# A 32-byte tile in front and two padded tiles: every tile of an attention and expert kernel moves in SBUF

## The chip, the cores and the metric

The kernel runs on one core of a Trainium2 chip. The metric is the device time of one execution in microseconds (us). Before the change it is 664.34 us, the median of 3 runs (664.32 to 665.79).

## What is computed

The reference is a linear attention with complex decay over 4 batches, 8 heads, 768 steps and 48 dimensions, followed by a mixture of 8 experts on its output.

```python
for t in range(S):                       # a = a_re + i a_im, scaled to a magnitude of at most 0.999
    new_re = ar * S_re - ai * S_im
    new_im = ar * S_im + ai * S_re
    S_re, S_im = (new_re + kv, new_im)   # kv = outer(k[t], v[t])
    y[t] = q[t] @ S_re
x = y as [3072 tokens, 384]
noisy_logits = x @ w_gate + log1p(exp(x @ w_noise)) * noise
# each token goes to its two best experts, with softmax weights over the two
out[mask] += top2_w * (maximum(x[mask] @ w1[e], 0) @ w2[e])   # w1[e]: 384x1024, w2[e]: 1024x384
```

## The kernel before, in words

**Attention (the first 250 us or so).** The 768 steps are cut into 6 groups of 128, so with 4 batches there are 24 tiles. Running sums of the logarithm and the angle of the decay are matmuls with triangular constants (`tri_t`, `tri_l`, `mask`; L365, L389), queries and keys are turned by transposes against `ident` (L414), scores are matmuls (L425), and outputs add the scores' part and the state's (L478, L476). Each output tile is turned back (L491), a gate picks two experts for each token, and POOL scatters the tokens' rows `xr` into the experts' slots `xs` in DRAM (L570). The order of all these instructions on each engine is written out by hand in `ORDER`.

**Experts (from about 271 us).** Every expert has 832 slots, cut into a window 0 of 320 and a window 1 of 512. For an expert the kernel loads its rows into `xga` and `xgb`, turns them, and keeps them as `x0` and `x1` (one tile for each third of the 384 dimensions). [...]

- First product, L763 (`mm1`): for each of 8 blocks f of the hidden size, 9 matmuls add up in PSUM. The stationary operand is `w1` (128 columns of it), the moving one is `x1` (512 columns; 448 for expert 0) or `x0` (320 columns; 256 where an expert's last 64 slots of window 0 are empty, which the kernel asks at run time). So a window has 72 matmuls. ACT takes the maximum with zero into `h` (L772), DVE the rest of it (L776).
- Second product, L832 (`mm2`): an output tile j of 128 slots adds up 24 matmuls. The stationary operand is 128 columns of `h0` (tiles 0, 1) or `h1` (tiles 3 to 6), the moving one 384 columns of `w2`. Tile 2 has 64 slots and 16 matmuls (L838), and only where those slots are used; for expert 0 tile 6 is such a half tile too. DVE weighs and adds the result into `ao` (L846), and POOL sends it to the output's rows (L847).

The order on PE from expert 2 on: first product of window 1, first product of window 0, second product of tiles 3 to 6, then (2,) 0 and 1.

**Where tiles lie.** A tile takes the same bytes in each of the 128 partitions, rounded up to a multiple of 32. Pools on the left side stack up from byte 8,320 of a partition: the constants (`cp`) up to 21,216; behind it `pf` (the attention's working tiles), later replaced by `mp0`; then `mp1` and `mp2` for the experts. Pools on the right side (`pa`, `pq`: queries, keys, values, scores, `xr` and more) end at the top, whatever stands on the left. A new pool's tile that lies over a tile of a closed pool waits for that one's last reader. Positions before, as the remainder of the first byte on division by 64:

| tiles | pool | first byte | remainder |
|---|---|---|---|
| ident, tri_t, tri_l, mask, tri_b, ones_b, none, xga | cp | 8,320 to 13,248 | 0 |
| zero, wg, nz | cp | 18,080 to 20,384 | 32 |
| re, im, t0, ee, tf | pf | 21,216 to 73,440 | 32 |
| raw (loaded weights) | mp0 | 21,216 to 29,408 | 32 |
| w1 of even-numbered experts | mp0 | 33,504 to 61,792 | 32 |
| x0, h0 | mp0 | 41,824 to 83,808 | 32 |
| w2 | mp1 | 86,368 to 107,872 | 32 |
| w1 of odd-numbered experts | mp1 | 110,944 to 131,424 | 32 |
| ao, xgb, lim | mp2 | 135,520 to 152,672 | 32 |
| lo, x1, ex, h1, xt | mp2 | 152,704 to 202,240 | 0 |
| all larger tiles | pa, pq | 87,744 to 225,728 | 0 |

The slices that the matmuls take of `w1`, `w2`, `x` and `h` begin whole multiples of 256 bytes behind their tile's first byte, so they have the tile's remainder.

Of the kernel before, what the change touches and what calls it, by code (L numbers as in the profile page):

```python
# [9 lines left out]
F32 = mybir.dt.float32  # L10
# [67 lines left out]
def kernel(  # L78
# [14 lines left out]
    E = w_gate.shape[1]  # L93
# [16 lines left out]
    xd = nc.dram_tensor("xd", [N, DM + E], F32, kind="Internal").ap()  # L110

    cp = ctx.enter_context(tc.tile_pool(name="cp", bufs=1))

    def ones_where(t, cmp, pattern, cm, base, fill):
        nc.gpsimd.affine_select(out=t, in_=t, pattern=pattern, compare_op=cmp, fill=fill,
                                base=base, channel_multiplier=cm)
# [171 lines left out]
    def key(name, ins):  # L288
        K.setdefault(name, []).append(ins)
        return ins  # L290
# [322 lines left out]
    def load_x(e, w, dst):  # L613
        if w == 0 and e not in TAILS:
            ds = [key(f"S14.{e}{w}", nc.sync.dma_start(dst[:, 0:2], x3[e, 0:256].rearrange("(p j) r -> p j r", j=2))),
                  key(f"S14.{e}{w}", nc.sync.dma_start(dst[0:64, 2], x3[e, 256:320]))]
            first.extend(ds)
            for d in ds:
                for s in late:
                    tc.declare_no_dep(d.ins, s.ins, reason="slots behind the first 320")  # L620
        elif e == 0:
            key(f"S14.{e}{w}", nc.sync.dma_start(dst, x3[e, 320:CAP].rearrange("(j p) r -> p j r", p=128)))
        else:

            n = WIN[w][1]
            x = blocks(dst, n)
            o = CAP - n if w == 0 or e not in TAILS else 0
            for a in range(4):
                asked.append(nc.sync.dma_start(x[32 * a:32 * a + 32], x3[e, o:o + n, 96 * a:96 * a + 96].rearrange("(t p) r -> p t r", p=32)))
            if w == 0:  # L630
                return
            EX[e] = ex = mt([128, 7, 16], F32, name="ex", bufs=2)
            m = 6 if e in TAILS else 4
            asked.append(nc.sync.dma_start(ex[:, 0:m], x3[e, o:o + 128 * m, DM:ROW].rearrange("(m p) r -> p m r", p=128)))
            if e in TAILS:
                nc.sync.dma_start(ex[0:64, 6], x3[e, CAP - 64:CAP, DM:ROW])

    def blocks(t, n):
        return t.rearrange("p j r -> p (j r)")[:, 0:3 * n].rearrange("p (t r) -> p t r", r=96)
# [15 lines left out]
    W1, W2, XW, HT, GW, OX, EX, DONE = {}, {}, {}, {}, {}, {}, {}, {}  # L655
    where = {}

    def mt(shape, dt, name, **kw):

        at_ = len(mpools) - 1  # L660
        if name.startswith(("raw", "h0", "x0", "gw", "ox")) or name.startswith("w1") and name.endswith("0"):
            at_ = 0
        elif name.startswith(("w1", "w2")):
            at_ = 1
        return where.setdefault(name, mpools[at_]).tile(shape, dt, name=name, **kw)
# [240 lines left out]
    for g in range(NG):  # L906
        for lo, hi in ((0, B),) if g < NG - 2 else ((0, B - 1), (B - 1, B)):
            for f, k, x in ((glog, 0, "gl"), (gturn, 2, "gl"), (gpick, 4, "gd"), (gdis, 10, "gd")):
                at(pos(B * g + hi + .5 + P[x], f"G{k}.{part(g, lo)}"), f, g, lo, hi)
            at(pos(behind_key(B * g + hi + .5 + P["gd"], f"G12g.{part(g, lo)}"), f"S13.{part(g, lo)}"), gscat, g, lo, hi)  # L910
        if g == NG - 4:
            at(pos(behind_key(B * g + hi + .5 + P["gd"], f"G12g.{g}"), "S14.00"), load_x, 0, 0, xga)
# [36 lines left out]
    for kk in range(KD):  # L949
        at(max(fpos + .002, PLACE[f"P21.00{kk}"]), x_T, 0, 0, (kk,))  # L950
        at(max(qpos + .003, PLACE[f"P21.10{kk}"]), x_T, 1, 0, (kk,))
    at(max(fpos + .003, PLACE["S14.10"], PLACE[f"P21.00{KD - 1}"] + .001), load_x, 1, 0, xga)
    for f in range(KF):
        at(PLACE[f"P22.00{f}"], mm1, 0, 0, (f,))
# [21 lines left out]
    mp = mpools[-1]  # L976
# [3 lines left out]
    xgb = mp.tile([128, 4, ROW], F32, name="xgb")  # L980
    for a in ao:
        nc.vector.memset(a, 0.0)
    lim = mp.tile([128, E], F32, name="lim")
    nc.gpsimd.iota(lim, pattern=[[N, E]], base=CAP, channel_multiplier=0, allow_small_or_imprecise_dtypes=True)
    load_x(0, 1, xgb)
    mm2(0, 0)
    ON = {"G0": "P", "G1": "A", "G2": "P", "G5": "A", "G7": "A", "G9": "A", "G10": "P"}
# [239 lines left out]
```

## Time and profile before

| | |
|---|---|
| time, median of 3 runs | 664.34 us |
| profiled execution | 671.12 us, span 669.3 us |
| PE busy | 633.1 us, 95% of the span |
| weight load (PEld) busy | 566.3 us, 85% |
| DVE busy | 430.4 us, 64% |
| ACT busy | 327.5 us, 49% |
| POOL busy | 175.6 us, 26% |
| granted TensorE clock, mean | 0.994 |

The span is the time from the first to the last instruction of the profiled execution. PEld is TensorE's load of a stationary operand, which runs beside the matmul before it. Matmuls overlap, so the distance between their starts tells what one costs, not its duration in the trace.

### The profile page before, as it was taken

Reading aid. Unit: us, or ns where it says so; the run is one execution under the profiler, and the core shown is the slowest. Engines: PE = TensorE matmul, PEld = TensorE weight load, DVE = VectorE, ACT = ScalarE, POOL = GpSimd, SP = SyncE. Lnnn points to the kernel's source line nnn. Section 1 sums busy time; section 2 is a strip of 40 time slices with the busy share of each in tenths; the row PEclk is TensorE's granted clock in tenths of the full one; section 3 lists DMA queues with packets and bytes.
Section 4 is the critical chain, followed back from the end, with each engine's and each line's share of the span. In section 5 each row is a group of like instructions: output and inputs, shape, how many; then the busy total and the mean of one; then the engine's idle time right before and its main releaser. Section 6 shows DMA issues by size and latency. Waiting matters only on the chain.

```text
span 669.3 us, 13780 instructions
## 1 busy us (share of the span) xinstructions
PE 633.1 (95%) x5312; PEld 566.3 (85%) x5312; DVE 430.4 (64%) x957; ACT 327.5 (49%) x556; POOL 175.6 (26%) x185
## 2 busy tenths in 40 slices
PE   1599999999999999999999999999999999999995
PEld 0378788888688979898998998998998999999995
DVE  7789999999987578445465535736545744634311
ACT  7799989999954633314233403504413504503300
POOL 3000004242614136016124124024123312312311
PEclk9999999999999999999999999999999999999998
DMA  8588875756596366815647157156355725401211
GB/s 263 161 286 253 230 205 177 227 174 162 173 267 190 103 210 210 209 37 150 168 107 191 58 131 233 49 144 209 96 109 166 188 65 156 142 36 60 69 37 35
DMA packets 97049, 102.68 MB, mean 153 GB/s; under 512 B 60815, under 2 KB 78096, under 8 KB 96968
## 3 DMA queue, kind: packets, MB, share of 16 engines
q1 hardware_dynamic: 87624, 74.08, 40.2%
q0 software_dynamic: 9344, 27.54, 11.6%
q8 instruction: 48, 0.79, 0.5%
q14 instruction: 33, 0.27, 0.1%
HBM read 70.93 MB, written 31.60 MB: 153 GB/s over the span
## 4 chain that ended last, share of the span: by engine, by line
PE 83%; ACT 6%; DVE 4%; DMA 3%; issue 2%; POOL 0%; another core or an unknown queue 0%; SPq 0%; POOLq 0%; ACTq 0%; DVEq 0%
PE po L832 30%; PE ph L763 28%; PE ptr L414 4%; PE psc L425 4%; PE cum L365 2%; PE pY L476 2%; PE pY L478 2%; PE pG L439 2%; ACT t L296 2%; PE po L838 2%; PE psc L763 2%; PE cum L389 2%; PE cum L491 1%; PE cum L503 1%; ACT ee L296 1%
## 5 line engine op out<-in xcount | busy, mean ns | idle before, releaser
L832 PE MATMUL po<-w2h,h 128*128 128x384 f32 x752 | 194.6, 337 | 0.0
L763 PE MATMUL ph<-x,w1h 128*128 128x512 f32 (+3 forms) x720 | 185.5, 346 | 0.4 <-issue 0.4
L763 PEld LDWEIGHTS ph<-x,w1h 128*128 128x128 f32 x720 | 126.0, 188 | 16.8 <-DVE ox L726 0.8
L832 PEld LDWEIGHTS po<-w2h,h 128*128 128x128 f32 x752 | 136.7, 188 | 0.1
L832 PE MATMUL po<-w2l,h 128*128 128x384 f32 x376 | 126.7, 337 | 0.0
L763 PE MATMUL ph<-x,w1l 128*128 128x512 f32 (+3 forms) x360 | 124.4, 345 | 0.0
L847 POOL DMA_INDIRECT out_dram<-ao,ox x52 | 52.5, 1009 | 255.9 <-DVE ao L846 200.7
L776 DVE SCALAR_TENSOR_TENSOR h<-ph,h 128x256 fp32r<-128x256 f32 (+3 forms) x152 | 69.6, 481 | 67.3 <-ACT h L772 51.6
L570 POOL DMA_INDIRECT xs<-xr,sl x48 | 57.5, 1198 | 185.6 <-DMA im<-in_a_dram 93.1
L772 ACT ACTIVATE h<-ph 128x512 fp32r<-128x512 f32 (+2 forms) x112 | 55.6, 502 | 98.6 <-PE ph L763 86.1
L846 DVE SCALAR_TENSOR_TENSOR ao<-po,ex,ao 128x384 f32<-128x384 f32 (+1 forms) x42 | 25.8, 615 | 87.8 <-PE po L832 87.5
L763 PEld LDWEIGHTS ph<-x,w1l 128*128 128x128 f32 x360 | 67.9, 188 | 7.9
L832 PEld LDWEIGHTS po<-w2l,h 128*128 128x128 f32 x376 | 70.6, 188 | 0.1
L685 ACT CAST w2h<-raw 128x768 fp32r<-128x768 f32 x32 | 26.3, 833 | 84.2 <-PE po L832 73.8
L807 POOL DMA_INDIRECT ao<-out_dram,ox x49 | 55.5, 1134 | 37.1 <-DMA out_dram<-ao,ox 20.8
L743 ACT CAST x<-xt 128x512 fp32r<-128x512 f32 (+1 forms) x39 | 20.9, 546 | 54.1 <-DVE xt L742 52.2
L425 PEld LDWEIGHTS psc<-qT,kT 112*64 112x64 f32 x768 | 36.2, 137 | 6.5 <-issue 5.4
L425 PE MATMUL psc<-qT,kT 112*64 112x128 f32 (+1 forms) x768 | 41.2, 251 | 0.4 <-issue 0.3
L686 DVE TENSOR_TENSOR w2l<-raw,w2h 128x768 fp32r<-128x768 f32 x32 | 30.2, 955 | 12.9 <-ACT w2h L685 12.0
L478 PE MATMUL pY<-am,v 128*48 128x128 f32 x384 | 36.6, 273 | 0.9 <-DVE am L427 0.5
L427 DVE TENSOR_TENSOR am<-psc,mask 128x512 f32<-128x512 f32 x48 | 32.3, 682 | 6.2 <-PE psc L425 2.6
L296 ACT ACTIVATE t<-t 128x768 f32<-128x768 f32 (+1 forms) x42 | 31.6, 763 | 1.9 <-DVE bad L339 1.7
(227 smaller groups left out, 938.8 us busy)
## 6 DMA issues: line engine op xcount, KB each, us to landing
raw<-in_moe_w_dram SPq DMA_DIRECT2D x24, 512.0 KB
raw<-in_moe_w_dram SPq DMA_DIRECT2D x32, 384.0 KB
qk<-in_qk_dram SPq DMA_DIRECT2D x24, 384.0 KB
v<-in_v_dram SPq DMA_DIRECT2D x24, 288.0 KB
xgb<-xs SPq DMA_DIRECT2D x28, 192.0 KB
out_dram<-zero SPq DMA_DIRECT2D x12, 384.0 KB
re<-in_a_dram SPq DMA_DIRECT2D x11, 384.0 KB
im<-in_a_dram SPq DMA_DIRECT2D x11, 384.0 KB
```

The lines of the kernel that those rows point to most:

```text
L296: phases[i].append(nc.scalar.activation(*args, **kw))
L425: key(f"P5{'ab'[half]}.{n}", nc.tensor.matmul(p[o:o + 64, j, s:], KT[n][:, h, s:s + 64], QT[n][:, h, s:], start=True, stop=True, skip_grou ...
L427: LAST['am'] = nc.vector.tensor_mul(AM[n][:, 4 * half:4 * half + 4, :].rearrange("p (i r) t -> p i r t", r=2), p.rearrange("p (i r) t -> p ...
L478: x = nc.tensor.matmul(o, V[n][:, H + i if r else h, :], AM[n][:, h, :], start=not g, stop=True, skip_group_check=True)
L570: d = key(f"L{b}{kk}.{part(g, lo)}", nc.gpsimd.indirect_dma_start(out=xs, out_offset=bass.IndirectOffsetOnAxis(ap=sl[:, kk, b:b + 1], axis=0),
L686: d = key(f"D{name}", nc.vector.tensor_tensor(lo, raw_t, hi.bitcast(F32), op=OP.subtract))
L763: LAST['m'] = key(f"P22.{e}{w}{f}", nc.tensor.matmul(p[:, :c], W1[e, kk][i][:, f * 128:(f + 1) * 128], XW[w, kk][:, j, 0:c], start=(m == 0 ...
L772: key(f"A24.{e}{w}{f}", nc.scalar.activation(h[:, 0:c], p[:, :c], AF.Relu))
L776: LAST['h'] = key(f"D25.{e}{w}{f}", nc.vector.scalar_tensor_tensor(h[:, dst:dst + b - a], p[:, a:b], 0.0, h[:, hi:hi + b - a].bitcast(F32) ...
L807: nc.gpsimd.indirect_dma_start(out=ao[j][0:w, :], out_offset=None, in_=out, in_offset=bass.IndirectOffsetOnAxis(ap=OX[e][0:w, j:j + 1], ax ...
L832: LAST['po'] = key(f"P23.{e}{j}", nc.tensor.matmul(p[:, :DM], HT[w, f][i][:, o:o + 128], W2[f // 2][k2][:, f % 2, :], start=(m == 0), stop ...
L847: d = nc.gpsimd.indirect_dma_start(out=out, out_offset=bass.IndirectOffsetOnAxis(ap=OX[e][0:n, j:j + 1], axis=0), in_=a, in_offset=None, b ...
```

## The change

Three tiles get another size, and nothing else is touched: no instruction, no order, no queue.

```diff
     cp = ctx.enter_context(tc.tile_pool(name="cp", bufs=1))
+    cp.tile([128, 8], F32, name="gap")
...
-            EX[e] = ex = mt([128, 7, 16], F32, name="ex", bufs=2)
+            EX[e] = ex = mt([128, 8, 16], F32, name="ex", bufs=2)
...
-    lim = mp.tile([128, E], F32, name="lim")
+    lim = mp.tile([128, 32 * E], F32, name="lim")[:, 0:E]
```

`gap` is 32 bytes at the very start of `cp` and is never written or read. All tiles of the left side behind it move up by 32 bytes: the remainders 0 and 32 in the rows of `cp`, `pf`, `mp0`, `mp1` and of `ao`, `xgb` and `lim` change places. `lim` grows from 32 to 1,024 bytes and each of the two buffers of `ex` from 448 to 512. So `lo`, `x1` and the first `ex` move up by 1,024 bytes, the second `ex` by 1,088, `h1` and `xt` by 1,152, and their remainder stays 0. Tiles of the right side stay where they are. Only the first 8 numbers of `lim` and the first 7 blocks of `ex` are used, as before.

## Rows read from the trace of the kernel before

**Rows 1.** The page's table of engines: busy us, share of the span, instructions.

```profile
PE 633.1 (95%) x5312; PEld 566.3 (85%) x5312; DVE 430.4 (64%) x957; ACT 327.5 (49%) x556; POOL 175.6 (26%) x185
```

**Rows 2.** The page's costliest groups: xcount | busy, mean ns of one | idle before.

```profile
L832 PE MATMUL po<-w2h,h 128*128 128x384 f32 x752 | 194.6, 337 | 0.0
L763 PE MATMUL ph<-x,w1h 128*128 128x512 f32 (+3 forms) x720 | 185.5, 346 | 0.4 <-issue 0.4
```

**Rows 3.** The chain of waits from 269 us on: start us, us, what.

```profile
269.31 1.66 PE po L737 x12
270.97 16.00 PE ph L763 x81
286.97 12.71 PE po L832 x72
...
560.36 25.19 PE ph L763 x144
585.55 25.28 PE po L832 x144
610.83 25.44 PE ph L763 x144
636.27 25.30 PE po L832 x144
661.60 0.63 DVE ao L846
662.56 0.91 POOL out_dram L847
```

**Rows 4.** One window over the experts: us, busy us of each engine (xinstructions), PEclk, DMA, GB/s.

```profile
270.97:661.57 390.60, 390.17 (x2164) 365.29 (x2162) 193.16 (x341) 119.33 (x204) 104.79 (x98) 1.00 0.43 120
```

**Rows 5.** Windows of L832, experts 6 and 5: tiles 3 to 6, then 0 and 1.

```profile
585.39:602.33 16.94, 16.94 (x96) 16.94 (x97) 1.00 0.10 36
602.33:610.66 8.33, 8.33 (x50) 8.19 (x48) 1.00 0.14 49
534.92:551.87 16.95, 16.95 (x96) 16.95 (x97) 1.00 0.22 65
551.87:560.19 8.32, 8.32 (x49) 8.17 (x48) 1.00 0.14 49
```

**Rows 6.** Windows of L763: expert 7 (512, 256), 6 (512, 256), 4 (320), 0 (448).

```profile
610.67:627.46 16.79, 16.79 (x72) 13.50 (x73) 1.00 0.35 103
627.47:636.10 8.63, 8.63 (x73) 8.59 (x71) 1.00 0.00 1
560.20:576.89 16.69, 16.69 (x72) 13.51 (x73) 1.00 0.82 250
576.90:585.38 8.48, 8.48 (x73) 8.44 (x71) 1.00 0.15 47
470.89:481.39 10.50, 10.50 (x73) 10.40 (x71) 1.00 0.32 95
272.13:286.80 14.67, 14.67 (x74) 13.35 (x72) 1.00 0.84 205
```

**Rows 7.** The chain of waits inside the attention: transposes, then running sums.

```profile
108.67 0.87 PE ptr L414 x8
109.54 1.30 PE cum L365 x4
```

**Rows 8.** Groups of PE by line and shape: matmuls that read ident.

```profile
L414 PE MATMUL ptr<-ident,kh 128*112 128x128 f32 x192 | 26.3, 281 | 4.2 <-ACT qT L415 4.2
L414 PE MATMUL ptr<-ident,qh 128*112 128x128 f32 x192 | 25.4, 275 | 1.1 <-DVE qh L404 0.6 <-ACT kT L415 0.4
L491 PE MATMUL cum<-ident,xT 128*128 128x128 f32 x96 | 14.7, 280 | 0.0
```

**Rows 9.** Groups of DVE by line and shape, 768 wide.

```profile
L404 DVE TENSOR_TENSOR qh<-qk,tr 128x768 f32<-128x768 f32 x24 | 22.8, 948 | 0.0
L394 DVE TENSOR_TENSOR qk<-qk,ee 128x768 f32<-128x768 f32 x24 | 22.7, 949 | 0.7 <-ACT ee L296 0.6
L338 DVE TENSOR_TENSOR t<-im,t 128x768 f32<-128x768 f32 x10 | 9.5, 951 | 0.2 <-ACT t L296 0.2
```

**Rows 10.** The chain of waits between the last scatter and the experts.

```profile
260.02 0.98 POOL xs L570
...
261.30 2.60 DMA xs<-xr,sl
263.90 0.02 issue
...
264.38 4.89 DMA xgb<-xs
```

**Rows 11.** What the value tiles' last readers are: duration ns min/median/max, first and last start.

```profile
L478 PE MATMUL pY<-am,v x384: 269/272/310, 37.8 to 244.6; 128*48 128x128 f32 x192
```

## The prediction, made before the changed kernel ran

> **What bounds the kernel now.** I read the page's table of engines first: PE is busy 95% of the span, the next engine 64% [rows 1]. The list of costly groups puts the experts' two matmul lines on top, and the idle time in front of them is 0.0 to 0.4 us [rows 2]. The chain of waits then shows where that matters: from 270.97 us on it consists of those two lines and the half tiles (L838), one expert behind the other, until the last product goes out [rows 3]. [...] So after 271 us the time is the number of expert matmuls times the distance from one start to the next. Before 271 us PE shares the path with ACT, DVE and transfers.
>
> No instruction is added or removed. All that changes is where tiles lie, so the question is whether that distance depends on it. The profile has an answer, because the tiles already lie in two kinds of places. I call a position odd if it leaves 32 on division by 64, even if it is a multiple of 64. Window rows over one expert's stretches, divided by the matmuls the code puts there (counts in the rows include one or two under way at an edge):
>
> - Second product, tiles 3 to 6 (stationary h1, even; moving w2, odd): 96 matmuls of 384 columns in 16.94 and 16.95 us, 176.5 ns each [rows 5].
> - Second product, tiles 0 and 1 (stationary h0, odd; moving w2, odd): 48 of the same shape in 8.33 and 8.32 us, 173.4 ns each [rows 5].
> - First product, window 1 (stationary w1, odd; moving x1, even): 72 matmuls of 512 columns in 16.79 us with an odd-numbered expert's w1, 233.2 ns, in 16.69 with an even-numbered one's, 231.8 ns; 448 columns 14.67 us, 203.8 ns [rows 6].
> - First product, window 0 (stationary w1, odd; moving x0, odd): 256 columns in 8.63 us, 119.9 ns, and 8.48 us, 117.8 ns; 320 columns 10.50 us, 145.8 ns [rows 6].
>
> [...]
>
> **The change part by part.** *The 32 bytes in front* make w1, w2, x0 and h0 even; *the two paddings* keep x1, h1 and xt even. Afterwards no expert matmul has mixed operands. [...] Then:
>
> - second product, tiles 3 to 6: 7 experts x 96 + 72 for expert 0 = 744 matmuls x 3.1 ns = 2.3 us;
> - window 1 with 512 columns: 288 (experts 1, 3, 5, 7) x 6.6 ns + 216 (experts 2, 4, 6) x 5.2 ns = 1.9 + 1.1 us; with 448 columns (expert 0): 72 x 3.8 ns = 0.3 us;
> - second product, tiles 0 to 2 and the half tiles (464 matmuls), window 0 (576): odd with odd becomes even with even, 0.
>
> The sum is 5.6 us. All of it lies behind 270.97 us, since x1 and h1 aren't multiplied earlier, on a stretch where PE waits for nothing; per expert of some 50 us it is 0.7 us. Next in line there is DVE, busy 193.16 of 390.60 us [rows 4], so nothing takes the place of the time that goes.
>
> *The constants become odd.* ident is the moving operand of 480 transposes (2 x 192 + 96 [rows 8]) whose stationary operands stay even. That mixes them. [...] I take 0.
>
> *DVE and ACT.* The 768-wide DVE operations take 948 ns with all tiles even, 949 with qk even and ee odd, 951 with all odd [rows 9]: 0.
>
> *Transfers.* Tiles that transfers write move by 32 bytes too. The trace doesn't separate transfers by position; the one on the path before the experts is xgb, 4.89 us [rows 10]. A tenth of it either way, 0.5 us, is my bound; I take 0.
>
> *Other overlaps.* The paddings push x1, ex, h1 and xt up by 1,024 to 1,152 bytes over other tiles of the attention, whose last reader they must await. The value tiles are last read by matmuls that begin at 244.6 us [rows 11], x1 is first filled after 269; the gathered rows xr are last read by the scatters that end by 263.90 [rows 10], h1 is first written after 270.97. More than 7 us to spare in the tighter case: 0. The iota on lim has no one queued behind it who is on the path.
>
> The sum is made on the profiled execution: 671.12 us around a span of 669.3, so 665.5 after. The median of the runs shown is 664.34, 6.8 us lower; the matmul distances at full clock are the same thing in both, so I take the 5.6 us off the median: 658.7 us.
>
> [...]
>
> **The rivals.**
>
> 1. *No change.* h0 and h1 differ in more than the half of 64 bytes: h1 and x1 lie 20 to 130 KB further up than w1 and w2, and the slow pairs are just those that reach across. If the distance makes the price, it stays: 664.3 us. For it: the same pairs are mixed and far apart. Against it: the w1 of odd-numbered experts lies 20 to 55 KB below x1, that of the others 90 to 130 KB, and the nearer ones are the slower (16.79 us against 16.69). And within one kind of pair, another position within 512 bytes changes the price (even against odd experts, 8.48 against 8.63 us), which distance doesn't explain.
>
> [...]
>
> [...]
>
> **How the numbers follow.** Forecast 0.53, no change 0.17, even better as such 0.17, even slower 0.13. A difference under 0.3%, 2.0 us, can't be told from none. Faster takes the forecast and the second rival but for a rest that falls short of 2.0 us: 0.69. Same 0.17. Slower the third and the transposes' 1.4 us with no gain beside them: 0.14. The forecast's own range is 656.5 to 661. For 8 in 10 the range reaches down to 646, half of the second rival, and up to 666, no change plus 1.4 us for the transposes; the far end of the second and most of the third stay outside.
>
> **What would show it.** Right: in the changed trace the windows of tiles 3 to 6 and of tiles 0 and 1 both come to 173 to 174 ns a matmul, the 512-column ones to about 227, while 256 columns stay at 120 and the DVE durations stand. Rival 1: 176.5 and 233 again. [...] Wrong also if the experts' stretch shortens and the attention's end comes later by as much.

## The result and the profile after

The changed kernel takes 660.02 us (median of 7 runs, 659.49 to 661.45) against 665.89 us before (7 runs on the same chip): a ratio of 0.991, 95% interval 0.989 to 0.993, or 5.9 us less. The forecast was 5.6 us less. The profiled execution is 660.58 us around a span of 658.8. The operations are those of before; all lines behind L112 have a number higher by one (L764 is L763 of before, L833 is L832).

The chain of waits of the changed kernel from the experts on (start us, us, what):

```profile
265.67 15.93 PE ph L764 x81
281.60 12.50 PE po L833 x72
...
551.11 25.16 PE ph L764 x144
576.27 24.96 PE po L833 x144
601.24 25.00 PE ph L764 x144
626.23 24.98 PE po L833 x144
651.24 0.63 DVE ao L847
```

It is the same chain as [rows 3], shorter piece by piece: 24.96 for 25.28 us of second product, 25.00 for 25.44 of an odd-numbered expert's first product. One window over it (us, busy us of PE, PEld, DVE, ACT, POOL, granted clock, DMA share, GB/s):

```profile
265.67:651.24 385.57, 385.53 (x2163) 363.16 (x2162) 193.46 (x342) 119.91 (x204) 105.28 (x98) 1.00 0.42 122
```

385.57 us stand where 390.60 stood [rows 4], so the experts give 5.0 us. Their start is 5.3 us earlier too, but that is not shown to be the edit's doing. The profiled execution of before took 671.12 us around a span of 669.3, longer than any of the 7 runs beside the change; a run with the same two figures stands among the 14 runs of before on the chip of e1 to e3, whose median is 670.40. The experiments below show that the part ahead of the experts differs by that much between chips, for kernels whose attention is the same.

Now the same stretches as in [rows 5, 6], second product first (experts 6 and 5: tiles 3 to 6, tiles 0 and 1), then the first (expert 7: 512 and 256 columns, expert 6: the same, expert 4: 320, expert 0: 448):

```profile
576.11:592.74 16.63, 16.63 (x96) 16.63 (x97) 1.00 0.10 36
592.75:601.07 8.32, 8.32 (x49) 8.17 (x48) 1.00 0.15 51
525.98:542.62 16.64, 16.64 (x96) 16.64 (x97) 1.00 0.23 66
542.62:550.94 8.32, 8.32 (x49) 8.17 (x48) 1.00 0.13 49
601.08:617.43 16.35, 16.35 (x72) 13.51 (x73) 1.00 0.35 105
617.44:626.06 8.62, 8.62 (x73) 8.58 (x71) 1.00 0.00 1
550.95:567.59 16.64, 16.64 (x72) 13.55 (x73) 1.00 0.80 246
567.60:576.10 8.50, 8.50 (x73) 8.46 (x71) 1.00 0.17 57
462.70:473.22 10.52, 10.52 (x73) 10.42 (x71) 1.00 0.31 94
266.83:281.43 14.60, 14.60 (x74) 13.34 (x72) 1.00 0.78 206
```

Divided by their 96, 48 or 72 matmuls: tiles 3 to 6 came from 176.5 to 173.3 ns, tiles 0 and 1 stayed at 173.3, 512 columns of odd-numbered experts came from 233.2 to 227.1. But 512 columns of even-numbered experts went only from 231.8 to 231.1 and 448 columns from 203.8 to 202.8, where 226.6 and 200.0 were forecast. The stretches that the forecast put at 0 are where they were.

The attention's transposes with ident odd, and the DVE operations of [rows 9] (busy us, mean ns of one):

```profile
108.75 0.87 PE ptr L415 x8
109.62 1.30 PE cum L366 x4
```

```profile
L405 DVE TENSOR_TENSOR qh<-qk,tr 128x768 f32<-128x768 f32 x24 | 22.8, 950 | 0.0
L395 DVE TENSOR_TENSOR qk<-qk,ee 128x768 f32<-128x768 f32 x24 | 22.7, 950 | 0.7 <-ACT ee L297 0.6
L339 DVE TENSOR_TENSOR t<-im,t 128x768 f32<-128x768 f32 x10 | 9.5, 950 | 0.2 <-ACT t L297 0.2
```

0.87 and 1.30 us are the figures of [rows 7], and the transposes of [rows 8] have mean durations of 282, 276 and 280 ns where they had 281, 275 and 280: the constants' move shows no price there. Nor does the move of DVE's operands: 950 ns each, where [rows 9] have 948, 949 and 951.

### The profile page after: what moved, and what is told of

It is laid out like the page before. It is cut to its first block, busy times and chain, and to the rows that moved or that the text cites. A ratio compares the mean times of both kernels' runs of the same rounds, so it can differ in the third digit from the quotient of the medians.

```text
span 658.8 us, 13781 instructions
## 1 busy us (share of the span) xinstructions
PE 625.9 (95%) x5312; PEld 563.3 (86%) x5312; DVE 430.4 (65%) x957; ACT 328.0 (50%) x556; POOL 178.0 (27%) x185
## 4 chain that ended last, share of the span: by engine, by line
PE 81%; ACT 7%; DVE 5%; DMA 3%; issue 2%; POOL 1%; SPq 0%; POOLq 0%; DVEq 0%; ACTq 0%
PE po L833 30%; PE ph L764 28%; PE ptr L415 4%; PE psc L426 3%; PE pY L477 2%; PE pY L479 2%; PE cum L366 2%; ACT t L297 2%; PE po L839 2%; PE psc L764 2%; PE cum L390 1%; PE pG L440 1%; PE cum L492 1%; ACT L296 1%; ACT ee L297 1%
## 5 line engine op out<-in xcount | busy, mean ns | idle before, releaser
L833 PE MATMUL po<-w2h,h 128*128 128x384 f32 x752 | 192.7, 335 | 0.0
L764 PE MATMUL ph<-x,w1h 128*128 128x512 f32 (+3 forms) x720 | 184.2, 344 | 0.0
L764 PEld LDWEIGHTS ph<-x,w1h 128*128 128x128 f32 x720 | 126.2, 189 | 14.5
L833 PEld LDWEIGHTS po<-w2h,h 128*128 128x128 f32 x752 | 135.9, 188 | 0.1
L833 PE MATMUL po<-w2l,h 128*128 128x384 f32 x376 | 125.7, 334 | 0.0
L764 PE MATMUL ph<-x,w1l 128*128 128x512 f32 (+3 forms) x360 | 124.0, 344 | 0.0
L571 POOL DMA_INDIRECT xs<-xr,sl x48 | 59.3, 1236 | 177.2 <-DVE t L342 92.9
L764 PEld LDWEIGHTS ph<-x,w1l 128*128 128x128 f32 x360 | 67.9, 189 | 7.2
L833 PEld LDWEIGHTS po<-w2l,h 128*128 128x128 f32 x376 | 70.6, 188 | 0.1
L477 PE MATMUL pY<-qT,z 112*48 112x128 f32 x320 | 31.8, 276 | 0.9 <-DVE z L462 0.9
```

What stands on the lines that cost most here:

```text
L477: x = nc.tensor.matmul(o, Z[b][:, h, :], QT[n][:, h, :], start=True, stop=False, skip_group_check=True)
L571: d = key(f"L{b}{kk}.{part(g, lo)}", nc.gpsimd.indirect_dma_start(out=xs, out_offset=bass.IndirectOffsetOnAxis(ap=sl[:, kk, b:b + 1], axis=0),
L764: LAST['m'] = key(f"P22.{e}{w}{f}", nc.tensor.matmul(p[:, :c], W1[e, kk][i][:, f * 128:(f + 1) * 128], XW[w, kk][:, j, 0:c], start=(m == 0 ...
L833: LAST['po'] = key(f"P23.{e}{j}", nc.tensor.matmul(p[:, :DM], HT[w, f][i][:, o:o + 128], W2[f // 2][k2][:, f % 2, :], start=(m == 0), stop ...
```

## The experiments

The theory on record was that a price comes where one operand is odd and the other even. Its rivals were that even is good as such, and that distance over many KB makes the price. The first two experiments put the tiles into the other combinations.

**e1_all_odd: x1 and h1 made odd instead of the rest even.**

```diff
-    lim = mp.tile([128, E], F32, name="lim")
+    lim = mp.tile([128, 2 * E], F32, name="lim")[:, 0:E]
```

> Nothing in front, ex as before; lim alone grows from 32 to 64 bytes, so that x1, ex and h1 move by 32 bytes and lie odd like w1, w2, x0 and h0: like operands everywhere, all of them odd, and the constants stay even. Theory (the price comes from one operand even and the other odd, whichever): tiles 3 to 6 at 173.4 ns a matmul, 512 columns at 226.7 ns for odd-numbered experts, the experts' stretch some 5 us shorter than before, ratio 0.991. Rival (even positions are what helps): tiles 3 to 6 lose their even h1, 173.4 at best, 512 columns stay at 233 or rise, ratio 0.996 to 1.003. Rival (distance of 20 to 130 KB): all as before, 176.5 and 233, ratio 1.00.

Measured: ratio 0.9954 (0.9938 to 0.9970, 9 runs), 666.75 us where before is 670.4 on that chip. Windows of expert 7 and 6 with 512 columns, then tiles 3 to 6 of expert 6:

```profile
606.23:622.70 16.47, 16.47 (x72) 13.52 (x73) 1.00 0.35 105
556.07:572.74 16.67, 16.67 (x72) 13.54 (x73) 1.00 0.78 246
581.24:597.88 16.64, 16.64 (x96) 16.64 (x97) 1.00 0.10 36
```

Tiles 3 to 6 fall to 173.3 ns with everything odd: even is not what made the 173.3, and the distance in KB, unchanged, did not keep the 176.5. But 512 columns come to 228.8 ns, not 226.7 (231.5 for even-numbered experts), and the ratio of 0.991 that the theory expected lies outside the interval.

**e2_gap_alone: the 32 bytes in front and ex's padding, without lim's.**

```diff
-    lim = mp.tile([128, 32 * E], F32, name="lim")[:, 0:E]
+    lim = mp.tile([128, E], F32, name="lim")
```

(against the changed kernel, as are the following)

> The changed kernel with lim back at its 32 bytes: the tile of 32 bytes in front and ex as changed, so w1, w2, x0 and h0 are even, x1 and h1 odd. Theory (mixing): tiles 3 to 6 at 176 to 177 ns again and 512 columns at 230 to 233, tiles 0 and 1 at 173.4, time as before, ratio 0.999 to 1.001. Rival (even positions help as such): w1 and w2 are even, so about half of the 5 us stays, ratio 0.995. Rival (the moves of about 1,000 bytes matter, not the half): x1 and h1 have nearly their old distance to w1 and w2, as before too, but by that rule e1_all_odd changes nothing either.

Measured: ratio 0.9959 (0.9946 to 0.9972), experts' stretch 387.65 us. Expert 7 and 6 with 512 columns, tiles 3 to 6:

```profile
607.43:624.22 16.79, 16.79 (x72) 13.50 (x73) 1.00 0.35 103
557.25:573.94 16.69, 16.69 (x72) 13.51 (x73) 1.00 0.82 254
582.44:599.09 16.65, 16.65 (x96) 16.65 (x97) 1.00 0.10 36
```

Here h1 is odd and w2 even, and the second product still takes 173.4 ns. My theory falls: here a mixed pair does not pay. The first product stays at 233.2 and 231.8, to the hundredth of a microsecond what [rows 6] have, with both operands 32 bytes further up.

That suggested another theory, to be tried on these matmuls: *the price follows from the distance between the two operands, taken modulo some hundred bytes.* In the kernel before w1 less x1 leaves 224 on division by 256, in e2 as well; in the changed kernel it leaves 0, in e1 192. For h1 less w2 the remainders are 160 before, 0 after, 192 in e1, 32 in e2.

**e3_one_phase: the even-numbered experts' w1 brought to the same distance.** In the changed kernel a third of their w1 tiles leaves 128 and the others 0, because gw and ox (128 bytes) lie between them.

```diff
-            GW[e] = mt([128, 8], F32, name="gw", bufs=2)
+            GW[e] = mt([128, 32], F32, name="gw", bufs=2)[:, 0:8]
...
-            OX[e] = mt([128, 8], U32, name="ox", bufs=2)
+            OX[e] = mt([128, 32], U32, name="ox", bufs=2)[:, 0:8]
```

> The changed kernel with gw and ox at 128 bytes a buffer instead of 32 (384 bytes more in front of x0), so that the w1 parts of even-numbered experts all leave the same remainder on division by 512 as those of odd-numbered ones; in the changed kernel one third of them leaves 256 and the others 384. Theory (position inside 512 bytes matters below the even/odd rule): 512 columns of even-numbered experts fall from 231.3 to 226.7 ns, 216 x 4.6 ns = 1.0 us less than the changed kernel; their 256 columns rise from 118.0 to 120.0 ns, 72 x 2 = 0.1 us more; ratio to before 0.990. Rival (w1 of even-numbered experts lies further from x1, 90 to 130 KB, and that is their price): 231.3 and 118.0 stay, ratio 0.991.

Measured: ratio 0.9923 (0.9910 to 0.9936), where 0.990 was expected. 512 columns, experts 7 and 6:

```profile
605.74:622.09 16.35, 16.35 (x72) 13.52 (x73) 1.00 0.34 105
555.78:572.13 16.35, 16.35 (x72) 13.52 (x73) 1.00 0.77 241
```

Both kinds of expert take 227.1 ns now. What the even-numbered ones had kept was their third of tiles at another distance, not their place 90 to 130 KB below x1. The figure is the same at a DMA share of 0.34 and of 0.77.

The first product of window 0 goes the other way, as the expectation has it. In the changed kernel a third of expert 6's w1 also leaves 128 on division by 256 when x0 is taken away from it, and its 256 columns take 8.50 us; in e3 all of it leaves 0, and they take 8.62, as expert 7's do in the changed kernel:

```profile
572.14:580.76 8.62, 8.62 (x73) 8.58 (x71) 1.00 0.22 73
```

So beside e3 the third at 128 goes with dearer 512 columns (231.1 for 227.1 ns) and cheaper 256 columns (118.1 for 119.7 ns).

**e4 to e8: the distance scanned.** e3 with lim longer, so that x1 and h1 move up together and the rest stays. Only the number differs:

```diff
-    lim = mp.tile([128, 32 * E], F32, name="lim")[:, 0:E]
+    lim = mp.tile([128, 32 * E + 16], F32, name="lim")[:, 0:E]   # e4; e5: + 32, e6: + 64, e7: + 48, e8: + 8
```

> e3_one_phase with lim 64 bytes longer: x1 and h1 stay even, but their distance to w1 and w2 inside 512 bytes is 192 instead of 256. Theory (beyond the even/odd rule only a mix of distances costs): 512 columns 226.7 ns, tiles 3 to 6 173.3. Rival (the distance inside 512 bytes has a price of its own): either figure moves by 1 ns or more.

> e3_one_phase with lim 128 bytes longer: every first product of window 1 and every second product of tiles 3 to 6 has its stationary and moving operand at a distance that leaves 128 on division by 512 (first product: w1 less x1 is 128; second: h1 less w2 is -128, which leaves 384). All positions stay even. New theory (the price follows from that distance alone, odd or even don't matter): figures unlike e3_one_phase's 226.7 and 173.3, namely 228 to 233 and 174 to 177 ns. Old theory (mixing odd and even costs, nothing else): 226.7 and 173.3.

> e3_one_phase with lim 256 bytes longer: the distance leaves 0 on division by 512 in all products, as it does already in tiles 0 and 1. New theory: second product 173.3 as tiles 0 and 1; first product 226.7 if the pattern repeats every 256 bytes, something else if it repeats every 512. Old theory: 226.7 and 173.3.

> e3_one_phase with lim 192 bytes longer: w1 less x1 leaves 64 on division by 512, h1 less w2 leaves 448. New theory: if the pattern repeats every 256 bytes, these are the same as 320 and 192: second product 173.4 (as in e1_all_odd at 192). First product unknown at 320, 226 to 234. Old theory: 226.7 and 173.3.

> e3_one_phase with lim 32 bytes longer: x1 and h1 odd, w1 and w2 even; w1 less x1 leaves 224, h1 less w2 leaves 288. New theory: first product 233.3 for every expert, the even-numbered ones too (the distance of 224 that the odd-numbered had before), second product 173.5 (as in e2_gap_alone at 288). Old theory: first product 233 for odd-numbered, second product 176.5.

Each of the five ran once, so their times are not compared; the distances are read from the windows of their traces, first 512 columns of expert 7, then tiles 3 to 6 of expert 6. e4, and under it tiles 3 to 6 of expert 4:

```profile
607.34:623.81 16.47, 16.47 (x72) 13.52 (x73) 1.00 0.35 105
582.22:599.00 16.78, 16.78 (x97) 16.78 (x98) 1.00 0.09 36
481.59:498.55 16.96, 16.96 (x97) 16.96 (x97) 1.00 0.42 108
```

e5:

```profile
610.20:626.99 16.79, 16.79 (x72) 13.52 (x73) 1.00 0.34 103
584.96:601.85 16.89, 16.89 (x96) 16.89 (x97) 1.00 0.09 36
```

e6:

```profile
606.81:623.16 16.35, 16.35 (x72) 13.51 (x73) 1.00 0.35 104
581.84:598.48 16.64, 16.64 (x96) 16.64 (x97) 1.00 0.09 36
```

e7:

```profile
606.73:623.52 16.79, 16.79 (x72) 13.54 (x73) 1.00 0.33 103
581.75:598.40 16.65, 16.65 (x97) 16.65 (x98) 1.00 0.09 36
```

e8, with 512 columns of expert 6 under those of expert 7:

```profile
608.50:625.28 16.78, 16.78 (x72) 13.49 (x73) 1.00 0.34 103
558.06:574.85 16.79, 16.79 (x72) 13.50 (x73) 1.00 0.79 249
583.50:600.15 16.65, 16.65 (x96) 16.65 (x97) 1.00 0.09 36
```

e4's first expectation, 226.7 and 173.3 ns, failed and its rival came true; the figures of e5, e7 and e8 agree with the new theory and not with the old, those of e6 with both. All kernels together, ns a matmul, by what the distance leaves on division by 256:

| remainder | 512 columns (w1 less x1) | 384 columns, tiles 3 to 6 (h1 less w2) |
|---|---|---|
| 0 | 227.1 (changed, e3, e6) | 173.3 (changed, e3, e6) |
| 32 | | 173.4 (e2, e8) |
| 64 | 233.2 (e7) | 174.8 to 176.7 (e4) |
| 128 | 233.2 (e5) | 175.9 (e5, e9) |
| 160 | | 176.5 (before) |
| 192 | 228.8 (e1, e4) | 173.4 (e1, e7) |
| 224 | 233.2 (before, e2, e8) | |

(odd-numbered experts of before, e1, e2 and the changed kernel, whose w1 is all at one distance; any of e3 to e8.) Each remainder but one has one figure in a column, whether the operands are both even, both odd or mixed: 228.8 is both odd in e1 and both even in e4; 233.2 is mixed in e8 and even in e5. e6 leaves 0 on division by 512 and e3 leaves 256, with the same figures; h1 less w2 leaves 448 in e7 and 192 in e1, 384 in e5 and 128 in e9, again with the same figures. So in these rows distances that are 256 bytes apart have the same figure; more was not tried. In e8 the even-numbered experts pay as the odd-numbered ones, once all their w1 is at 224. Two things the distance does not settle. In e4 tiles 3 to 6 take 176.7 ns in expert 4, where the 16 matmuls of the half tile 2 (L839) run just before them, and 174.8 in expert 6, where the first product does; whether what runs just before is the cause, no run shows. And the rows are for tiles that are all at one distance: in the changed kernel's even-numbered experts, with a third at 128 and the rest at 0, 512 columns take 231.1 ns and not the mean of (233.2 + 2 x 227.1) / 3 = 229.1.

**e9_ex_as_before: the padding of ex taken back.** ex was a multiple of 64 bytes before, so for odd and even this edit does nothing.

```diff
-            EX[e] = ex = mt([128, 8, 16], F32, name="ex", bufs=2)
+            EX[e] = ex = mt([128, 7, 16], F32, name="ex", bufs=2)
```

> The changed kernel with ex back at 448 bytes a buffer: h1 moves down by 128 bytes, all positions stay even, h1 less w2 leaves 128 on division by 512 instead of 256. Theory (the price follows from the distance of the two operands modulo 256): second product of tiles 3 to 6 at 176.0 ns as in e5_dist_128, first product as in the changed kernel, so 744 x 2.7 ns = 2.0 us of the gain are lost, ratio 0.994 to 0.995. Old theory (odd against even): 173.3, nothing lost, ratio 0.991.

Measured: ratio 0.9955 (0.9939 to 0.9970) beside 0.9923 for the changed kernel on the same chip. Expert 7, 512 columns; tiles 3 to 6 of expert 6:

```profile
602.61:618.97 16.36, 16.36 (x72) 13.52 (x73) 1.00 0.35 105
577.37:594.26 16.89, 16.89 (x96) 16.89 (x97) 1.00 0.10 36
```

175.9 ns, as the new theory has it. Without ex's 128 bytes the change would have lost most of its gain in the second product (175.9 ns of 176.5 before and 173.3 after), though every tile that its matmuls read would lie on a multiple of 64 bytes.

**e10 and e11: the changed kernel and e3 side by side.**

> The changed kernel once more, beside e11 on one chip, so that the two can be compared: ratio to before 0.991 to 0.993.

> The kernel of e3_one_phase beside the changed one: 512 columns of even-numbered experts at 226.7 instead of 231.3 ns, 1.0 us less, 0.1 us more in the 256 columns of expert 6; ratio to before lower than that of e10_changed_again by 0.001 to 0.002. Rival (the attention's part pays for the 384 bytes): no lower.

Measured: 0.9923 (0.9909 to 0.9936) and 0.9934 (0.9909 to 0.9958), medians 660.17 and 660.02 us. The intervals can't tell them apart. The traces do for the experts, by their first and last line in the chain of waits; e10:

```profile
264.55 15.93 PE ph L764 x81
...
650.12 0.63 DVE ao L847
```

e11:

```profile
264.60 15.90 PE ph L764 x81
...
649.67 0.63 DVE ao L847
```

385.57 against 385.07 us, 0.5 us less, where 0.9 was expected. Some 0.3 us of the 0.9 went in expert 2's first product, which is longer in e11 than expert 4's of the same shape, as it is not in the changed kernel; e11, experts 2 and 4:

```profile
340.05:367.23 27.18, 27.18 (x144) 23.89 (x144) 1.00 0.60 167
444.93:471.85 26.92, 26.92 (x144) 23.97 (x144) 1.00 0.58 182
```

That e11 takes less time as a whole is not shown.

The same difference of starts, 387.64 us in e9 and 387.65 in e2, stands for ratios near 0.9955 in both. On the chip of e9 to e11 the experts begin at 264.6 to 265.4 us, on the one of e1 to e3 at 270.2 to 270.7, with the same attention: that is the part of the span that differs between chips.

## Why the prediction was right, and which step was wrong

**The bound: right.** PE sets the time behind 270.97 us (after the change it is busy 385.53 of the stretch's 385.57 us), and the experts' stretch is 5.0 us shorter: 4.4 us as shorter distances between matmuls and some 0.7 us as a pause that only the profiled execution of before has (both below). Nothing became late in its place: DVE is busy 193.46 of 385.57 us. The medians differ by 5.9 us, and their interval reaches from 4.4 to 7.3, so the rest is no more than the runs scatter.

**The reading of the rows: wrong.** The failed step is the reading that a pair of one even and one odd operand costs 3 to 7 ns more: in e2 the second product has such a pair and takes 173.4 ns. That the price belongs to the pair was right: moving both by 32 bytes changes nothing (first product, 16.79 us in before and in e2), nor does moving both by 384 (odd-numbered experts, 16.35 us in the changed kernel and in e3). But odd or even was a coincidence of two remainders, 224 and 160, which are both multiples of 32 and not of 64. What the figures go with in the table is the distance modulo 256: 227.1 and 173.3 ns at 0, while other multiples of 64 have up to 233.2 (e5, e7) and 175.9 (e5, e9). No run shows why. The change brought both products to remainder 0: x1 by the 32 bytes in front together with a lim that moves x1 by a whole 1,024, h1 by ex's further 128. That the tiles come to lie on multiples of 64 bytes is not why it helps: in e5 they do, with 233.2 and 175.9 ns.

**The terms of the sum.** No run shows the constant price a matmul from which the forecast took its 6.6, 5.2 and 3.8 ns; what the windows show in their place, after the change, is 6.1 ns less for 512 columns of odd-numbered experts, 0.7 for the even-numbered ones and 1.0 for 448 columns. Nor does one show the 1.4 us that the chances and the range allow for the transposes: 8 of them take 0.87 us before and after. The 646 us of the range, half of the second rival, was the author's estimate alone. Tiles 3 to 6: 744 matmuls x (16.95 - 16.64) us / 96 = 2.4 us, forecast 2.3. 512 columns, odd-numbered experts: 4 x (16.79 - 16.35) = 1.8, forecast 1.9. Even-numbered: 3 x (16.69 - 16.64) = 0.15, forecast 1.1; this term was mis-sized, because one third of that w1 stayed at another distance (e3 brings the rest). 448 columns: 0.07, forecast 0.3. Expert 0's half tile 6 reads h1 too and was counted among the terms at 0; its 16 matmuls take 2.91 us before and 2.87 after. Together 4.4 us. The rest of the 5.0 is a pause, where the prediction had PE waiting for nothing. In before the first product of expert 2 takes 27.89 us and that of expert 4, of the same shape, 27.21; after the change both take 27.18. The chain of before has the pause, and the timeline puts the wait of the next weight load down to DVE, which had itself waited 6.20 us for a transfer:

```profile
347.50:375.39 27.89, 27.47 (x144) 23.83 (x144) 1.00 0.61 163
454.19:481.40 27.21, 27.21 (x144) 23.91 (x144) 1.00 0.58 180
360.19 0.42 issue
359.67 0.17 DVE L724 CAST ox<-ex 128x4 uint32<-128x4 f32 x1 [6.20 <-DMA out_dram<-ao,ox]
360.60 0.30 PEld L763 LDWEIGHTS ph<-x,w1h 128*128 128x128 f32 x2 [0.85 <-DVE ox L726]
```

No other profiled execution shows PE idle there, the kernels with other distances included, so it is not shown to be a gain of the edit.

**How much of it was luck.** That 5.6 us came out so near is partly luck. The rule behind it expected some 5 us from e1 as well, where the experts' stretch went from 390.6 to 386.4 us, and nothing from e2, where it went to 387.65, each time with the 0.7 us of the pause in the difference. The changed kernel obeys the rule and, by the sizes of its pads, also brings the distances to 0; and the two terms that were too large by 1.2 us together are made up for by the pause and the scatter of the runs.

**Edits at nothing: right.** Constants and DVE cost nothing by their rows (0.87 and 1.30 us as before, DVE 950 ns for 948 to 951), and nothing in the chain of waits points at transfers or the new overlaps.

**The rivals.** "No change" by distance in KB is refuted by e1, where tiles 3 to 6 fall from 176.5 to 173.3 ns; "even better as such" and "even slower" by tiles 0 and 1, which go from both odd to both even and stay at 173.3 ns. The objection I raised myself against the first rival, that within one kind of pair another position within 512 bytes changes the price, was a first sight of what the experiments then found (256 columns at 117.8 and 119.9 ns before, 118.1 and 119.7 after); I used it against a rival and did not turn it against the forecast.

**The stationary operand alone.** With the moving tile where it was and the stationary one moved by 128 bytes (e9 against the changed kernel), a matmul goes from 173.3 to 175.9 ns. So the place of the weights matters here. Whether the load or the running matmul is held up, no row tells.

Left open: why the figures repeat at 256 bytes, and where some 12 ns a matmul come from that stay at remainder 0: an estimate from 119.7, 173.3 and 227.1 ns at 256, 384 and 512 columns, which lie on 12.3 ns and 0.4195 ns a column to within 0.1 ns. Attempts to load no weights between matmuls were not made.

## What to carry to other kernels

When a profile shows one shape of matmul at two speeds, list where both operands lie and compare their distance before their alignment: padding one tile is then a cheap trial, and the distance between two starts over a whole product, in a window of the trace, measures it to 0.1 ns. What a distance costs can differ with the number of columns, as it did here between 512 (231.1 for 227.1 ns) and 256 (118.1 for 119.7), so each shape wants its own window. A rule that fits all rows of one layout is still one layout: two pads that keep the rule and change the rest would have told here which rule it was. And an edit described as alignment can work through something else, so take its parts away one by one.

## What the runs showed of the hardware

At the granted clock of 1.00 the starts of the experts' matmuls lay 119.7, 173.3 and 227.1 ns apart at 256, 384 and 512 columns where the two operands' distance leaves 0 on division by 256 (e3: 8.62 us for 72, 16.64 for 96, 16.35 for 72). By these three a further column takes 0.42 ns. At 512 columns it was 233.2 ns at the worst (remainders 64, 128 and 224: e7, e5, before), 6.1 ns more. At 256 columns a third of the tiles at 128 made it less, 118.1 ns for 119.7 (changed kernel, expert 6 beside expert 7). The attention's transposes showed no price for a move of ident by 32 bytes, 0.87 us for 8 of them at either position; other distances were not tried there. Even with all w1 at one distance, 512 columns take 16.35 us for 72; by the estimate of some 12 ns a matmul, about 5% of that product's time remains beyond its columns.
